# Attention and feed-forward on one core: slots 8 to 31 as four written lists, tail keys as 64-row matmuls with a bank per head

## The chip, the cores and the metric

The kernel runs on one core of a Trainium2 chip. The metric is the device time of one execution in microseconds (us), here as the median of three runs. The engines of the core run side by side, each through its own queue in order: PE (TensorE, matmuls into PSUM, with PEld its weight loads), ACT (ScalarE), DVE (VectorE), POOL (GpSimd) and SP (SyncE). Work of one engine that needs another's result waits on a semaphore. PSUM is used here in units of one bank (512 float32 values in each of 128 partitions).

## The reference

Eight batches, eight heads, 576 positions of 64 values, attention with a bias by distance, then a feed-forward block in which two products are multiplied with each other:

```
scores = scale * np.matmul(q, k.transpose(0, 1, 3, 2))
scores = scores + bias.transpose(2, 0, 1)[None, :, :, :]
scores = scores - np.max(scores, axis=-1, keepdims=True)
attn = np.exp(scores)
attn = attn / (np.sum(attn, axis=-1, keepdims=True) + 1e-09)
attn_out = np.matmul(attn, v).astype(np.float32)
...
x = np.ascontiguousarray(attn_out.transpose(0, 2, 1, 3)).reshape(B * S, H * D)
a = x @ w_a
b = x @ w_b
return (a * b @ w_out).astype(np.float32)
```

x has 4608 rows of 512; w_a and w_b are 512 x 1536, w_out is 1536 x 512. Matmuls take bfloat16 operands.

## The kernel before, in words

**Units of attention.** The work goes in 32 pairs of heads, p = 0 to 31 (p // 4 is the batch, p % 4 the pair of heads in it). The 576 positions are four tiles of 128 (t, 512 "main" positions) and a tail of 64. Scores stand with keys on the partitions and queries along the row. The two heads of a pair (hh = 0 and 1) lie on partitions 0 to 63 and 64 to 127, so a score matmul uses 64 rows of the array.

For a pair p of 8 or more:
- `qk(p, t0)` makes main scores: per tile t two 64-row matmuls of 512 columns into a two-bank tile of pool `ps_sc` (two buffers). With t0 == 2 it also makes the "rows", the scores of main keys against the 64 tail queries: eight 64-row matmuls of 64 columns (L424), head 0 into the bank `trb`, head 1 into a bank of pool `ps_av`.
- `ex(p, t)` on ACT takes the exponential of two banks at once into `at` (L439), `ex_rows` that of the rows into `att` (L431). `mul` (L444) and `mul_rows` (L539) on DVE multiply by the exponential of the bias.
- `qk_tail(p)` makes the scores of tail keys (both heads, 128 rows; 512 and 128 columns, L488 and L489), `ex_tail` (L515) and `mul_tail` (L531) follow.
- `av_mm(p, jqs)` makes the weighted values for query tiles jq = 0 to 4 (4 is the tail): for each a matmul of 130 columns over the tail keys of both heads (L568; in `vt` each head's values stand on its own 64 partitions with zeros on the other 64), then four matmuls of 65 columns per head over the main keys (L578), or, for jq = 4, four of 130 columns (L572). Column 65 of each head holds ones, so it gives the sum for the division.
- `av_norm(p, jqs)` on DVE takes the reciprocals (L589) and multiplies into `XG` (L591, L596). `t_x(p)` has SP transpose `XG` into `xn_sb`, the input of feed-forward.

**Units of feed-forward.** A chunk of 512 rows is 36 units of four matmuls of 512 columns: 24 units (12 x a and b: `ff_in` L642, then on ACT a copy `ha` L649, or on DVE the product `g` L652) and 12 units of output (`ff_o_mm` L679, four row tiles of three units, then on ACT the copy `ob` L684 and the DMA to `out`). Their banks come from pool `ps_ff` (two buffers).

**Order.** The scheduler is off (`manual_schedule`): each engine runs in the order of the program text. An opening of written tokens does p = 0 to 7 and the first chunk's part. Then a loop over slots s = 8 to 32 (L868) does, in slot s, scores, exponentials and multiplies of p = s and weighted values of p = s - 1, in the order of `steps`; nine feed-forward units per slot are put where `U` stands, whole units, with ACT's and DVE's part of a unit right behind its matmuls. In a slot the weighted values stand in two blocks, jq 0 to 2 and jq 3 to 4. Slot 32 has no new scores. The rest of the units comes after the loop. Loads from DRAM (POOL's queue) and the transposes of a batch (SP's queue) are put at the start of certain slots.

Of the kernel before, what the change touches and what calls it, by code (L numbers as in the profile page):

```python
# [13 lines left out]
def kernel(  # L14
# [11 lines left out]
    nc = tc.nc  # L26
# [7 lines left out]
    NM = 4  # L34
# [370 lines left out]
    def shared(p):  # L405
        return p >= 8

    def qk(p, t0, ts=None):
        qT, kT, _ = operands(p)
        st[p].setdefault("at", [None] * NM)  # L410
        for t in ts or (t0, t0 + 1):
            ps = ps_sc.tile([128, 2, 512], FP32, tag="sc", name=f"qk{p}_{t}")
            for hh in range(2):
                r = slice(64 * hh, 64 * hh + 64)
                nc.tensor.matmul(out=ps[:, hh, :], lhsT=kT[r, t, :], rhs=qT[r, :, :],  # L415
                                 start=True, stop=True)
            st[p]["ps", t] = ps
        if shared(p) and t0 == 2:
            z = operands(p)[2]
            rows = (trb.bitcast(FP32), ps_av.tile([128, 512], FP32, tag="av", name=f"qr{p}"))  # L420
            for t in range(NM):
                for hh in range(2):
                    r = slice(64 * hh, 64 * hh + 64)
                    nc.tensor.matmul(out=rows[hh][:, ST * t:ST * t + ST], lhsT=kT[r, t, :],  # L424
                                     rhs=z[r, 0, ST * hh:ST * hh + ST], start=True, stop=True)
            st[p]["rows"] = rows
# [99 lines left out]
    def mul_tail(p):  # L526
        if not shared(p):
            mul_rows(p)
        at, wt = st[p]["att"], Wt_sb[:, p % 4, :]
        o = 512 + main_tail(p) - 128  # L530
        nc.vector.tensor_tensor(out=at[:, o:o + 256], in0=at[:, o:o + 256], in1=wt[:, 255::-1], op=MULT)  # L531

    def mul_rows(p):
        at, w = st[p]["att"], W_sb[p % 4]
        x = at[:, 0:512].rearrange("p (t h c) -> p h t c", h=2, t=NM)
        rev = w[:, :, ST - 1::-1]
        e = bass.AP(tensor=rev.tensor, offset=rev.offset,
                    ap=[rev.ap[0], rev.ap[1], [1, NM], rev.ap[2]])
        nc.vector.tensor_tensor(out=x, in0=x, in1=e, op=MULT)  # L539
# [19 lines left out]
    def av(p, jqs):  # L559
        av_mm(p, jqs)  # L560
        av_norm(p, jqs)

    def av_mm(p, jqs, pool=None, tag="av"):
# [16 lines left out]
                                     stop=True, skip_group_check=True)  # L580
        st[p]["pav", jqs[0]] = pav

    def av_norm(p, jqs):
        pav = st[p]["pav", jqs[0]]
        rc = wrk.tile([128, 3, 2], FP32, tag="rc", name=f"rc{p}_{jqs[0]}")
        xg = XG[p % 2]
        n = len(jqs)
        r = rc[:, 0:n, :]
        nc.vector.reciprocal(out=r, in_=pav[:, 0:n, :, Dh])  # L589
        m = n - (jqs[-1] == 4)  # L590
        nc.vector.tensor_tensor(  # L591
            out=xg[:, jqs[0]:jqs[0] + m, :, :], in0=pav[:, 0:m, :, 0:Dh],
            in1=rc[:, 0:m, :].unsqueeze(3).to_broadcast([128, m, 2, Dh]), op=MULT)
# [127 lines left out]
    def put_units(n):  # L721
        nonlocal nxt
        for _ in range(n):
            units[nxt]()
            nxt += 1

    def v_next(s):
        if s % 4 == 0:
            v_in(s // 4, 0, 4)
        if s % 4 == 2:  # L730
            v_in(s // 4, 4, 8)
# [132 lines left out]
        step(token)  # L864
    pad_tl(1)

    load_slot = {bb: 9 if bb == 3 else 12 if bb == 4 else 4 * bb - 5 for bb in range(3, B)}
    for s in range(8, NP + 1):  # L868
        new = s < NP
        U = "unit"  # L870
        A = lambda *jq: (lambda: av(s - 1, jq) if s > 8 else None)
        steps = []
        if new:
            steps += [lambda: (qk(s, 0), ex(s, 0))]
        if new:
# [12 lines left out]
        else:  # L888
            ff["late"] = True
            steps += [A(0, 1, 2), U, U, U, A(3, 4), lambda: t_x(s - 1, (0, 1, 2)), U, U, U,  # L890
                      lambda: t_x(s - 1, (3, 4)), U, U, U]
        b = s // 4 + 1
        if s % 4 == 2 and b < B:
            t_half(b, 0)
        if s % 4 == 0 and 2 <= b - 1 < B:
            t_half(b - 1, 1)
        if s % 4 == 1 and 2 <= b < B:
            load_vt(b)
        for bb in range(3, B):
            for g in range(2):  # L900
                if s == load_slot[bb] + (2 - (bb < 5)) * g:
                    load_half(bb, g)
        quota = 9
        seen, put = 0, 0
        nu = sum(1 for x in steps if x is U)
        for x in steps:
            if x is U:
                seen += 1
                n = (quota * seen + nu - 1) // nu - put
                put_units(n)  # L910
                put += n
            else:
                x()
    put_units(len(units) - nxt)


# [28 lines left out]
```

## Time and profile before

| What | Value |
|---|---|
| median of 3 runs | 413.77 us |
| lowest and highest run | 412.71 and 413.79 us |
| span of the profiled execution | 412.1 us |
| instructions in it | 8718 |
| slots 9 to 31, first score matmul to the next slot's | 11.00 to 11.01 us each |
| exponentials of main scores (L439), ACT | 112 x 1029 ns |
| multiplies of `at` (L444), DVE | 112 x 685 ns |
| 65-column weighted values (L578), PE | 896 x 193 ns from `at`, 128 from the opening's |
| tail-key weighted values (L568), PE | 152 x 221 ns from `att`, 8 from `atk` |

The span is the time from the first to the last instruction of one profiled execution. A matmul's duration in the profile includes its way through the array, on which the next one follows, so the duration is longer than what it takes of the engine's time: the distance from start to start tells that. Some matmul records are missing in the trace. Views used below: the page (busy shares, the clock granted to TensorE in 40 slices, the chain that ended last), the timeline (instructions in order of time, equal ones merged), the table of stages (busy time per engine in given stretches) and the list of waits.

### The profile page before, as it was taken

How to read it: one execution, taken by the hardware profiler on the slowest of the kernel's cores; microseconds unless marked ns; L12 is line 12 of the kernel's file. 1: busy time of each engine (PE TensorE's matmuls, PEld its weight loads, DVE VectorE, ACT ScalarE, POOL GpSimd, SP SyncE). 2: the span in 40 equal slices, each digit the busy share in tenths (PEclk: the TensorE clock that was granted, in tenths of full speed). 3: DMA queues.
4: the chain of work that ended last, by engine and by line, in shares of the span. 5: the costliest groups of instructions: out<-in, count | busy, mean ns of one | idle time of the engine just before them, and what ended most of it. 6: DMA issues, size and time to landing. Idle time of an engine off the chain costs nothing.

```text
span 412.1 us, 8718 instructions
## 1 busy us (share of the span) xinstructions
PE 401.5 (97%) x3420; PEld 209.6 (51%) x3471; DVE 240.6 (58%) x568; ACT 252.0 (61%) x386; POOL 131.4 (32%) x188
## 2 busy tenths in 40 slices
PE   7999999999999999999999999999999999999996
PEld 3476656455554555455445555555445454444443
DVE  4799997366755765476646764567547652421320
ACT  5898992577748665667557765767476642322321
POOL 5966466887029400960069004300000000000000
PEclk9999999999999999999999999999999999999999
DMA  9999999999969924994199908960520012002004
GB/s 152 185 204 197 206 137 148 166 184 131 91 127 157 141 40 91 151 127 94 35 159 150 120 17 136 117 92 17 117 67 17 16 40 78 0 5 98 2 2 102
DMA packets 135962, 42.36 MB, mean 103 GB/s; under 512 B 113544, under 2 KB 131176, under 8 KB 135920
## 3 DMA queue, kind: packets, MB, share of 16 engines
q0 software_dynamic: 81120, 19.88, 54.9%
q1 hardware_dynamic: 49456, 12.61, 19.9%
q10 hardware_dynamic: 5344, 9.31, 7.1%
q8 instruction: 27, 0.44, 0.5%
q14 instruction: 15, 0.12, 0.1%
HBM read 39.23 MB, written 9.45 MB: 118 GB/s over the span
## 4 chain that ended last, share of the span: by engine, by line
PE 95%; DMA 1%; ACT 1%; issue 1%; DVE 0%; ACTq 0%; SPq 0%
PE pb L642 23%; PE pa L642 23%; PE po L679 22%; PE av L578 8%; PE qk L415 7%; PE av L568 2%; PE av L572 2%; PE qkh L455 1%; PE qkt L488 1%; DMA xn<-in_k_dram 1%; PE trb L330 1%; PE trb L424 1%; PE trk L330 1%; ACT ath L461 0%; PE qkt L494 0%
## 5 line engine op out<-in xcount | busy, mean ns | idle before, releaser
L439 ACT ACTIVATE at<-qk 128x1024 bf16<-128x1024 f32 x112 | 113.4, 1029 | 27.4 <-DMA out_dram<-ob 10.3
L652 DVE TENSOR_TENSOR g<-pb,ha 128x512 bf16<-128x512 f32 (+1 forms) x114 | 75.6, 663 | 74.8 <-PE pb L642 58.5
L642 PE MATMUL pb<-xn,wb 128*128 128x512 bf16 (+1 forms) x440 | 111.1, 368 | 0.8
L642 PE MATMUL pa<-xn,wa 128*128 128x512 bf16 (+1 forms) x440 | 110.8, 368 | 0.7
L649 ACT ACTIVATE ha<-pa 128x512 f32<-128x512 f32 (+1 forms) x114 | 66.3, 581 | 67.6 <-PE pa L642 63.8
L679 PE MATMUL po<-wo,g 128*128 128x512 bf16 x403 | 95.5, 379 | 0.8
L444 DVE TENSOR_TENSOR at<-at,W 128x1024 bf16<-128x1024 bf16 x112 | 75.0, 685 | 22.4 <-ACT at L439 22.3
L642 PEld LDWEIGHTS <-wa 128*128 128x128 bf16 x456 | 41.2, 98 | 46.6 <-issue 6.8
L642 PEld LDWEIGHTS <-wb 128*128 128x128 bf16 x456 | 40.6, 98 | 42.9 <-issue 4.7
L679 PEld LDWEIGHTS <-g 128*128 128x128 bf16 x420 | 38.8, 98 | 44.9 <-issue 2.5
L684 ACT ACTIVATE ob<-po 128x512 f32<-128x512 f32 x34 | 20.4, 600 | 40.2 <-PE po L679 30.1
L578 PE MATMUL av<-vm,at 128*128 128x65 bf16 x896 | 41.2, 193 | 0.0
L578 PEld LDWEIGHTS <-at 128*128 128x128 bf16 x896 | 37.4, 97 | 6.1
L174 POOL DMA_DIRECT2D vt<-in_v_dram x12 | 7.4, 622 | 101.9 <-PE av L572 101.1
L136 POOL DMA_DIRECT2D qn<-in_q_dram x48 | 36.6, 825 | 9.2 <-PE trb L501 6.9
L589 DVE RECIPROCAL rc<-av 128x6 f32<-128x6 f32 (+1 forms) x64 | 11.9, 186 | 45.7 <-PE av L578 41.1
L145 POOL DMA_DIRECT2D kn<-in_k_dram x48 | 36.2, 800 | 2.6 <-DMA qn<-in_q_dram 1.6
L568 PE MATMUL av<-vt,att 128*128 128x130 bf16 x152 | 33.6, 221 | 0.2
L415 PE MATMUL qk<-QB,KB 64*128 64x512 bf16 x192 | 29.1, 381 | 0.3
L591 DVE TENSOR_TENSOR XG<-av,rc 128x384 bf16<-128x384 f32 (+2 forms) x64 | 27.2, 425 | 2.2
L515 ACT ACTIVATE att<-qkt 128x640 bf16<-128x640 f32 x24 | 16.8, 701 | 13.0 <-PE qkt L489 13.0
L568 PEld LDWEIGHTS <-att 128*128 128x128 bf16 x152 | 14.9, 98 | 6.4
(105 smaller groups left out, 322.8 us busy)
## 6 DMA issues: line engine op xcount, KB each, us to landing
out_dram<-ob ACTq DMA_DIRECT2D x31, 256.0 KB, 2.9
vn<-in_v_dram POOLq DMA_DIRECT2D x16, 256.0 KB, 5.7
kn<-in_k_dram POOLq DMA_DIRECT2D x48, 64.0 KB, 4.9
qn<-in_q_dram POOLq DMA_DIRECT2D x48, 64.0 KB, 4.1
wa<-in_moe_w_a_dram POOLq DMA_DIRECT2D x3, 512.0 KB, 8.9
wb<-in_moe_w_b_dram POOLq DMA_DIRECT2D x3, 512.0 KB, 8.3
wo<-in_moe_w_out_dram POOLq DMA_DIRECT2D x1, 1536.0 KB, 15.7
xn<-XG SPq DMA_TRANSPOSE x52, 3.5
```

What stands on the lines that cost most here:

```text
L136: nc.gpsimd.dma_start(out=by_tile(qn[b % 2])[:, h0 // 4, t, :, :], in_=q[b, h0:h1, 128 * t:128 * t + 128, :].transpose([1, 0, 2]))
L145: nc.gpsimd.dma_start(out=by_tile(kn[b % 2])[:, h0 // 4, t, :, :], in_=k[b, h0:h1, t:SM:NM, :].transpose([1, 0, 2]))
L415: nc.tensor.matmul(out=ps[:, hh, :], lhsT=kT[r, t, :], rhs=qT[r, :, :], start=True, stop=True)
L439: nc.scalar.activation(out=at[:, :, :], in_=ps[:, :, :], func=ACTF.Exp, scale=scale)
L444: nc.vector.tensor_tensor(out=at[:, :, :], in0=at[:, :, :], in1=w[:, :, S - 1 + t:S - 1 + t - SM:-1], op=MULT)
L568: nc.tensor.matmul(out=pav[:, slot, :, :], lhsT=weights_tail(p, jq), rhs=vt[i][:, :, hp, :], start=True, stop=True)
L578: nc.tensor.matmul(out=pav[:, slot, hh, :], lhsT=weights(p, t, hh, jq), rhs=vm[i][:, 2 * hp + hh, t, :], start=False, stop=True, skip_grou ...
L591: nc.vector.tensor_tensor(out=xg[:, jqs[0]:jqs[0] + m, :, :], in0=pav[:, 0:m, :, 0:Dh], in1=rc[:, 0:m, :].unsqueeze(3).to_broadcast([128, ...
L642: nc.tensor.matmul(out=ps[:, 0:n], lhsT=w[df // 4][:, mc, 128 * (df % 4):128 * (df % 4) + 128], rhs=xn_sb[mc][:, 512 * c + lo:512 * c + lo ...
L649: nc.scalar.activation(out=ha[:, 0:n], in_=ff["pa", df, lo][:, 0:n], func=ACTF.Copy)
L652: nc.vector.tensor_tensor(out=g_sb[df][:, lo:lo + n], in0=ff["pb", df, lo][:, 0:n], in1=ff["ha", df, lo][:, 0:n], op=MULT)
L679: nc.tensor.matmul(out=po[:, :], lhsT=g_sb[df][:, 128 * tt:128 * tt + 128], rhs=wo_sb[:, df, :], start=(df == 0), stop=(df == NDF - 1))
```

## The change

The loop over slots is replaced by four lists of tokens, `steady[s % 4]`, for s = 8 to 31. A token is one operation or a count of single matmuls: Qt scores of tile t, R the rows, K the tail keys' scores, E, ER, EK exponentials, M, MR, MK multiplies, TL the tail keys' weighted values, A so many matmuls of the other weighted values, Nh the normalisation of head h (with N1 also `t_x`), F so many feed-forward matmuls, H, G, O, D the copy `ha`, the product `g`, the copy `ob` and the output DMA of a unit, V the copy of values. A prime means p = s - 1.

The tail keys' weighted values (`av_tails`) become ten matmuls of 64 rows and 65 columns, head 0 into one bank and head 1 into another. The main keys' weighted values (`av_head`) are 40 matmuls of 65 columns, jq = 4 now per head too, first all of head 0, then of head 1, taken one by one between feed-forward matmuls. The two banks are the same as those of the rows (`two_banks`). Normalisation is per head (`norm_head`). p = 31 is still done by `av`, after the lists. In the new file the new matmuls are L595 (tails), L605 (others), L429 (rows), L942 and L949 (feed-forward), the new normalisation L614 to L618.

```diff
-    trb = ps_tr.tile([128, 1024], BF16, tag="tr", name="trb")
+    trb = [ps_tr.tile([128, 1024], BF16, tag="tr", name="trb")]
     turn = [0]
 
     def tr_half():
         turn[0] ^= 1
-        return trb[:, 512 * turn[0]:512 * turn[0] + 512]
+        return trb[0][:, 512 * turn[0]:512 * turn[0] + 512]
+
+    def two_banks(name):
+        return (ps_tr.tile([128, 512], FP32, tag="tr", name=f"{name}_0"),
+                ps_av.tile([128, 512], FP32, tag="av", name=f"{name}_1"))
...
-        if shared(p) and t0 == 2:
-            z = operands(p)[2]
-            rows = (trb.bitcast(FP32), ps_av.tile([128, 512], FP32, tag="av", name=f"qr{p}"))
-            for t in range(NM):
-                for hh in range(2):
-                    r = slice(64 * hh, 64 * hh + 64)
-                    nc.tensor.matmul(out=rows[hh][:, ST * t:ST * t + ST], lhsT=kT[r, t, :],
-                                     rhs=z[r, 0, ST * hh:ST * hh + ST], start=True, stop=True)
...
+    def qk_rows(p):
+        _, kT, z = operands(p)
+        st[p]["rows"] = rows = two_banks(f"qr{p}")
+        for t in range(NM):
+            for hh in range(2):
+                r = slice(64 * hh, 64 * hh + 64)
+                nc.tensor.matmul(out=rows[hh][:, ST * t:ST * t + ST], lhsT=kT[r, t, :],
+                                 rhs=z[r, 0, ST * hh:ST * hh + ST], start=True, stop=True)
...
+    J = Dh + 1
+
+    def av_tails(p):
+        b, hp = divmod(p, 4)
+        st[p]["av2"] = banks = two_banks(f"av{p}")
+        for jq in range(5):
+            for hh in range(2):
+                r = slice(64 * hh, 64 * hh + 64)
+                nc.tensor.matmul(out=banks[hh][:, J * jq:J * jq + J], lhsT=weights_tail(p, jq)[r, :],
+                                 rhs=vt[b % 2][r, hh, hp, :], start=(jq == 0), stop=True,
+                                 skip_group_check=True)
+
+    def av_head(p, hh):
+        b, hp = divmod(p, 4)
+        bank, v = st[p]["av2"][hh], vm[b % 2]
+
+        def mm(jq, t):
+            w = weights_last(p, t) if jq == 4 else weights(p, t, hh, jq)
+            return lambda: nc.tensor.matmul(out=bank[:, J * jq:J * jq + J], lhsT=w,
+                                            rhs=v[:, 2 * hp + hh, t, :], start=False, stop=True,
+                                            skip_group_check=True)
+
+        return [mm(jq, t) for jq in range(5) for t in range(NM)]
+
+    def norm_head(p, hh):
+        x = st[p]["av2"][hh][:, 0:5 * J].rearrange("p (j d) -> p j d", d=J)
+        rc = wrk.tile([128, 5], FP32, tag="rc2", name=f"rh{p}_{hh}")
+        nc.vector.reciprocal(out=rc[:, :], in_=x[:, :, Dh])
+        nc.vector.tensor_tensor(out=XG[p % 2][:, 0:4, hh, :], in0=x[:, 0:4, 0:Dh],
+                                in1=rc[:, 0:4].unsqueeze(2).to_broadcast([128, 4, Dh]), op=MULT)
+        rows = slice(ST * hh, ST * hh + ST)
+        nc.vector.tensor_tensor(out=XG[p % 2][0:ST, 4, hh, :], in0=x[rows, 4, 0:Dh],
+                                in1=rc[rows, 4:5].to_broadcast([ST, Dh]), op=MULT)
...
     def ff_o_out(c, tt):
+        ff_ob(c, tt)
+        ff_store(c, tt)
+
+    def ff_ob(c, tt):
         ob = ob_last if (c, tt) == (0, 2) else wrk.tile([128, DM], FP32, tag="ob", name=f"ob{c}_{tt}")
         nc.scalar.activation(out=ob[:, :], in_=ff["po", tt][:, :], func=ACTF.Copy)
+        ff["ob", tt] = ob
+
+    def ff_store(c, tt):
+        ob = ff["ob", tt]
...
+    steady = {
+        1: """
+            Q0 TL' Q1 A5 F1 A2 E0 A7 F1 A2 F1 A1 F1 A1 F1 H0 A2 F1 N0' A2 F1 E1 A2 F1 A3 F1 G1 A1
+            F1 A1 F1 A1 F1 M1 A7 H2 A2 F1 A1 F1 N1' F3 Q2 G3 Q3 E2 R M0 F4 H4 F3 E3 K G5 F3 M2 F2
+            H6 F1 M3 F2 EK F2 ER F1 MK F1 G7
+        """,
+        2: """
+            Q0 H8 Q1 MR' TL' E1 A5 F1 A2 F1 A1 F1 E0 A1 F1 A4 F1 G9 A4 F1 A2 F1 M1 A2 F1 A3 F1 H10
+            N0' A1 F1 A1 F1 A2 F1 A1 F1 A1 G11 A2 F1 A3 F1 A3 F1 A2 F1 H12 N1' F3 Q2 V Q3 G13 E2 R
+            F4 M2 F1 H14 F3 E3 K G15 F3 EK M0 F2 ER F1 MK F1 M3 H16
+        """,
+        3: """
+            Q0 Q1 MR' TL' A2 F1 A1 F1 A1 G17 A8 F1 A2 F1 A2 F1 A1 F1 H18 A3 F1 N0' A1 F1 E0 A2 F1
+            A2 F1 G19 A4 F1 E1 A4 F1 A5 F1 A2 F1 H20 N1' F3 Q2 G21 Q3 E2 R F1 M0 F3 M2 F1 H22 F2 K
+            E3 F3 G23 F1 EK F2 M1 ER F2 MK F1 M3 F2
+        """,
+        0: """
+            Q0 MR' Q1 TL' A3 F1 A2 F1 A1 F1 O26 A1 F1 A4 F1 E1 A2 F1 A2 F1 A2 F1 D26 A1 F1 A2 E0 F1
+            N0' A3 F1 A3 F1 A6 F1 A2 F1 A2 F1 O29 A2 F1 A1 F1 A1 D29 F1 N1' F3 Q2 M1 Q3 E2 R F4 ER
+            M2 F2 E3 K MR F1 V F2 M0 EK F3 O32 MK F1 M3 F2 D32 F2 O35 D35
+        """,
+    }
...
+    def ff_part(n):
+        c, u, m = 1 + (n // 4 - 48) // 36, (n // 4 - 48) % 36, n % 4
+        if u < 24:
+            df, (w, kind) = u // 2, ((wa_sb, "pa"), (wb_sb, "pb"))[u % 2]
+            if m == 0:
+                ff[kind, df, 0] = ff_bank(f"{kind}{c}_{df}")
+            nc.tensor.matmul(out=ff[kind, df, 0][:, :], lhsT=w[df // 4][:, m, 128 * (df % 4):128 * (df % 4) + 128],
+                             rhs=xn_sb[m][:, 512 * c:512 * c + 512], start=(m == 0), stop=(m == NMC - 1))
+        else:
+            tt, part = divmod(u - 24, 3)
+            if part == 0 and m == 0:
+                ff["po", tt] = ff_bank(f"po{c}_{tt}")
+            df = 4 * part + m
+            nc.tensor.matmul(out=ff["po", tt][:, :], lhsT=g_sb[df][:, 128 * tt:128 * tt + 128],
+                             rhs=wo_sb[:, df, :], start=(df == 0), stop=(df == NDF - 1))
+        if m == 3 and (u < 24 or u % 3 == 2):
+            ff["done"][u] = c
...
+    ff["skip"] = 108 - sum(int(x[1:]) for k in (1, 2, 3) for x in steady[k].split() if x[0] == "F")
+
+    def slot_step(s, token):
+        name, num = token.rstrip("'0123456789"), "".join(x for x in token if x.isdigit())
+        if name in ("F", "A"):
+            for _ in range(int(num)):
+                if name == "F" and ff["skip"] > 0:
+                    ff["skip"] -= 1
+                elif name == "F":
+                    ff_part(ff["mm"])
+                    ff["mm"] += 1
+                elif av_queue:
+                    av_queue.pop(0)()
...
+        if name == "Q":
+            qk(p, 0, (i,))
+        elif name == "TL":
+            av_tails(p)
+            av_queue[:] = av_head(p, 0) + av_head(p, 1)
+        elif name == "R":
+            qk_rows(p)
...
+        elif name == "N":
+            norm_head(p, i)
+            if i == 1:
+                t_x(p)
...
-    for s in range(8, NP + 1):
-        new = s < NP
-        U = "unit"
-        A = lambda *jq: (lambda: av(s - 1, jq) if s > 8 else None)
-        steps = []
-        if new:
-            steps += [lambda: (qk(s, 0), ex(s, 0))]
-        if new:
-            head = [U, lambda: ex(s, 1), A(0, 1, 2), U, lambda: mul(s, 0), U,
-                    lambda: mul(s, 1)]
-            late = [A(3, 4), lambda: t_x(s - 1), U]
-            if s == 8:
-                late = [U]
-            pair = [lambda: v_next(s), lambda: (qk(s, 2), ex(s, 2), ex_rows(s)), U,
-                    lambda: ex(s, 3), U, lambda: mul(s, 2), lambda: mul_rows(s)]
-            tail = [lambda: (qk_tail(s), ex_tail(s)), U, U, lambda: mul_tail(s)]
-            if s % 4 == 0:
-                steps += head + late + [U] + pair + [lambda: mul(s, 3)] + tail
-            else:
-                steps += head + pair + late + [U, lambda: mul(s, 3)] + tail
-        else:
-            ff["late"] = True
-            steps += [A(0, 1, 2), U, U, U, A(3, 4), lambda: t_x(s - 1, (0, 1, 2)), U, U, U,
-                      lambda: t_x(s - 1, (3, 4)), U, U, U]
+    while ff["skip"] < 0:
+        ff_part(ff["mm"])
+        ff["mm"] += 1
+        ff["skip"] += 1
+    for s in range(8, NP):
...
-        quota = 9
-        seen, put = 0, 0
-        nu = sum(1 for x in steps if x is U)
-        for x in steps:
-            if x is U:
-                seen += 1
-                n = (quota * seen + nu - 1) // nu - put
-                put_units(n)
-                put += n
-            else:
-                x()
+        for token in steady[s % 4].split():
+            slot_step(s, token)
...
+    nxt = ff["mm"] // 4
+    ff["late"] = True
+    trb[0] = ps_tr.tile([128, 1024], BF16, tag="tr", name="trz")
+    p = NP - 1
+    av(p, (0, 1, 2))
+    put_units(3)
+    av(p, (3, 4))
+    t_x(p, (0, 1, 2))
+    put_units(3)
+    t_x(p, (3, 4))
```

More of the change, by code (lines that the diff above doesn't have):

```diff
@@ L417, in qk @@
             st[p]["ps", t] = ps
-        if shared(p) and t0 == 2:
-            z = operands(p)[2]
-            rows = (trb.bitcast(FP32), ps_av.tile([128, 512], FP32, tag="av", name=f"qr{p}"))
-            for t in range(NM):
-                for hh in range(2):
-                    r = slice(64 * hh, 64 * hh + 64)
-                    nc.tensor.matmul(out=rows[hh][:, ST * t:ST * t + ST], lhsT=kT[r, t, :],
-                                     rhs=z[r, 0, ST * hh:ST * hh + ST], start=True, stop=True)
-            st[p]["rows"] = rows
+    def qk_rows(p):
[6 more added lines that the diff above has]
+                                 rhs=z[r, 0, ST * hh:ST * hh + ST], start=True, stop=True)
     def ex_rows(p):
@@ new lines @@
+    ff["done"] = {}
+    ff["mm"] = 4 * nxt
+    ff["skip"] = 108 - sum(int(x[1:]) for k in (1, 2, 3) for x in steady[k].split() if x[0] == "F")
[10 more added lines that the diff above has]
+                    av_queue.pop(0)()
+            return
+        if name in ("H", "G", "O", "D"):
+            u = int(num)
+            if u not in ff["done"]:
+                return
+            c = ff["done"][u] if name in ("H", "G", "O") else ff["done"].pop(u)
+            if name == "H":
+                ff_ha(c, u // 2, 0, 512)
+            elif name == "G":
+                ff_g(c, u // 2, 0, 512)
+            elif name == "O":
+                ff_ob(c, (u - 24) // 3)
+            else:
+                ff_store(c, (u - 24) // 3)
+            if name in ("H", "G"):
+                del ff["done"][u]
+            return
+        name, i = token.rstrip("'0123"), "".join(x for x in token if x.isdigit())
+        i = int(i) if i else 0
+        p = s - token.endswith("'")
+        if p < 8:
+            return
+        if name == "Q":
[5 more added lines that the diff above has]
+            qk_rows(p)
+        elif name == "K":
+            qk_tail(p)
+        elif name == "E":
+            ex(p, i)
+        elif name == "ER":
+            ex_rows(p)
+        elif name == "EK":
+            ex_tail(p)
+        elif name == "M":
+            mul(p, i)
+        elif name == "MR":
+            mul_rows(p)
+        elif name == "MK":
+            mul_tail(p)
+        elif name == "N":
+            norm_head(p, i)
+            if i == 1:
+                t_x(p)
+        elif name == "V":
+            v_next(p)
+        else:
+            raise ValueError(token)
@@ L892 @@
+    av_queue = []
+    load_slot = {bb: 9 if bb == 3 else 12 if bb == 4 else 4 * bb - 5 for bb in range(3, B)}
+    while ff["skip"] < 0:
[3 more added lines that the diff above has]
+    for s in range(8, NP):
         b = s // 4 + 1
@@ L902 @@
                     load_half(bb, g)
-        quota = 9
-        seen, put = 0, 0
-        nu = sum(1 for x in steps if x is U)
-        for x in steps:
-            if x is U:
-                seen += 1
-                n = (quota * seen + nu - 1) // nu - put
-                put_units(n)
-                put += n
-            else:
-                x()
+        for token in steady[s % 4].split():
+            slot_step(s, token)
+    for token in steady[0].split():
+        if token.endswith("'") and token[0] in "EM":
+            slot_step(NP, token)
+    while ff["mm"] % 4:
+        slot_step(NP, "F1")
+    for u in sorted(ff["done"]):
+        for name in (("O", "D") if u >= 24 else ("G",) if u % 2 else ("H",)):
+            slot_step(NP, f"{name}{u}")
+    nxt = ff["mm"] // 4
[8 more added lines that the diff above has]
+    t_x(p, (3, 4))
     put_units(len(units) - nxt)
```

## The prediction

> **What bounds the kernel now.** I read the page first (busy time, granted clock, the chain that ended last), then the waits of TensorE between 94 and 325 us, a table of four slots, and the timeline of one slot.
>
> ```profile
> PE 401.5 (97%) x3420; PEld 209.6 (51%) x3471; DVE 240.6 (58%) x568; ACT 252.0 (61%) x386; POOL 131.4 (32%) x188
> ...
> PEclk9999999999999999999999999999999999999999
> ...
> PE 95%; DMA 1%; ACT 1%; issue 1%; DVE 0%; ACTq 0%; SPq 0%
> ```
>
> TensorE is busy in 97% of the span at the full clock, and the chain of waits is TensorE in 95%. A matmul overlaps the next, so "busy" alone could hide pauses. The table of stages (engines' busy us, then clock, DMA share) is cut at the first score matmul of four slots in a row:
>
> ```profile
> 193.22:204.22 11.00, 10.89 (x94) 5.55 (x96) 7.48 (x17) 6.71 (x10) 0.00 (x0) 1.00 0.08 16
> 204.22:215.23 11.01, 10.90 (x94) 5.55 (x97) 4.76 (x12) 6.77 (x10) 5.49 (x8) 1.00 1.23 148
> 215.23:226.23 11.00, 10.95 (x95) 5.62 (x96) 7.36 (x18) 7.73 (x13) 11.00 (x17) 1.00 1.73 155
> 226.23:237.24 11.01, 10.90 (x94) 5.55 (x96) 7.54 (x18) 7.90 (x12) 0.54 (x1) 1.00 1.20 116
> ```
>
> Every slot takes 11.00 to 11.01 us whatever VectorE (4.8 to 7.5), ScalarE (6.7 to 7.9) and the DMAs do in it. The view of TensorE's waits between 94 and 325 us names no engine at all. So a slot is as long as its matmuls, and I price each by the distance from its start to the next start:
>
> ```profile
> 204.22 0.61 PE L415 MATMUL qk<-QB,KB 64*128 64x512 bf16 x4
> 204.76 1.04 PE L679 MATMUL po<-wo,g 128*128 128x512 bf16 x4
> 205.63 0.22 PE L568 MATMUL av<-vt,att 128*128 128x130 bf16 x1
> 205.69 0.42 PE L578 MATMUL av<-vm,at 128*128 128x65 bf16 x8
> 205.95 0.22 PE L568 MATMUL av<-vt,att 128*128 128x130 bf16 x1
> ...
> 206.33 0.42 PE L578 MATMUL av<-vm,at 128*128 128x65 bf16 x8
> 206.59 1.67 PE L679 MATMUL po<-wo,g 128*128 128x512 bf16 x7
> 208.31 0.22 PE L568 MATMUL av<-vt,att 128*128 128x130 bf16 x1
> ...
> 208.69 0.39 PE L572 MATMUL av<-vm,att 128*128 128x130 bf16 x4
> 208.92 1.89 PE L679 MATMUL po<-wo,g 128*128 128x512 bf16 x8
> 210.74 0.60 PE L415 MATMUL qk<-QB,KB 64*128 64x512 bf16 x4
> 211.19 0.19 PE L424 MATMUL trb<-ZB,KB 64*128 64x64 bf16 x1
> ...
> 211.28 0.19 PE L424 MATMUL qr<-ZB,KB 64*128 64x64 bf16 x1
> 211.40 1.90 PE L679 MATMUL po<-wo,g 128*128 128x512 bf16 x8
> ```
>
> The first four feed-forward matmuls last from 204.76 to 205.63: 0.216 each. Eight 65-column matmuls last from 205.69 to 205.95: 0.0325 each, also where a 512-column one follows (206.33 to 206.59). A 130-column tail matmul (L568) costs 0.06, one of L572 (208.92 - 208.69)/4 = 0.058. The eight 64-row matmuls of L424 start between 211.19 and 211.28: their pairs, one on each half of the rows, are 0.03 apart. Going from 64-row to 128-row work costs extra: four score matmuls from 204.22 to 204.76 are 0.54, where two pairs of 0.22 make 0.44. That is 0.1, and the return to 64 rows costs as much; a slot has four such changes.
>
> **The change, part by part.** It applies to the weighted values of p = 8 to 30, computed in slots 9 to 31: 23 slots. Slot 8 has none, p = 31 is done by the old function, and the opening and the closing feed-forward stay.
>
> Removed per slot: from the timeline, 205.63 to 206.59 and 208.31 to 208.92, together 0.96 + 0.61 = 1.57 us (5 of L568, 32 of L578, 4 of L572).
>
> Added per slot: 10 tail matmuls of 64 rows and 65 columns, which stand in alternation on the two halves and the two banks, like those of L424: 5 pairs of 0.03 = 0.15. And 40 matmuls of 128 rows and 65 columns (32 as before, 8 in place of the four wide ones) at 0.0325 = 1.30. Together 1.45.
>
> So 0.12 us less per slot, 23 x 0.12 = 2.8 us.
>
> Bounds. For the tails: no row shows 64 rows with 65 columns. Below, the pair distance of L424, 0.03; above, no overlap, ten at 0.03 each, 0.30. I take 0.03 a pair, since rows, halves and banks are as in L424. For the 65-column matmuls in the midst of feed-forward: the row of L578 is 0.0325 in a run and ahead of a 512-column one. Below, streaming alone: a 512-column one takes 0.216 and a 128-column one (L489, between feed-forward matmuls at 213.35 and 213.41) 0.056, so 0.42 ns a column and 0.030 for 65. Above, that 0.056. I take 0.0325, the same shape. For changes between 128 and 64 rows: the tails are put between or behind the first two score pairs, which are 64-row too, so there are still four a slot.
>
> The Trainium skill (TensorEngine Tiling, Key Properties) says that a change of tiling mode drains the array; the 0.1 us at each change agrees. It warns here against tails standing among 128-row work: by it two more changes a slot would cost 23 x 0.2 = 4.6 us, and the lists avoid them.
>
> The other parts cost or bring nothing by themselves. Feed-forward stays at 36 matmuls a slot on average (36, 35, 35 and 38 in the four lists). The mixing moves matmuls on an engine that never waits, so it has no wait to remove. VectorE has the same six normalising instructions for a pair; ScalarE's work and the loads keep their slots. The output DMA is issued on ScalarE some steps behind its copy; what stands behind is only ScalarE's, which idles 3 to 4 us a slot.
>
> New waits. Score rows (R) and weighted values now share one pair of banks. R is queued behind Q2 and Q3, and all matmuls behind R. It needs the second normalisation (N1') done. From the last weighted-value matmul to R's start lie 0.033, four feed-forward matmuls (0.86), a change (0.1) and Q2, Q3 (210.74 to 211.19, 0.45): 1.44 us. N1' needs 0.21 until that matmul's result is seen (L578 lasts 193 ns, 0.02 for the signal), a reciprocal (0.23, start to start on VectorE's timeline), a 256-column product (at most 0.47, the start-to-start of the 384-column one there), a 64-row product (0.22), and 0.07 to be seen by TensorE: 1.20. Slack 0.24 us if VectorE is free when N1' is due. In the reverse direction the tails (TL') wait for both exponentials of the rows. From Q2's end in list 1 ScalarE has E2, H4, E3, H6, the tail keys' and two row exponentials: by start-to-start distances on its timeline 0.90 + 0.49 + 0.90 + 0.49 + 0.6 + 0.53 = 3.9. TensorE has Q3, R, two changes, 19 feed-forward matmuls, the tail scores (0.27) and Q0: 0.22 + 0.12 + 0.2 + 4.1 + 0.27 + 0.22 = 5.1, so 1.2 are left for ScalarE's own waits in between. The closest place is H6 of list 1, queued behind E3: adding these distances along the list, the bank that it frees is wanted about 0.02 us after its end. If it is 0.05 late in each of the 6 slots of that list, that is 0.3 us, which I put in.
>
> Sum on the profiled execution: span 412.1 - 2.8 + 0.3 = 409.6. The runs took 412.71 to 413.79, so 0.6 to 1.7 lies around the span; the same difference on the median gives 413.77 - 2.5 = 411.3 us.
>
> **Rivals.**
> 1. The shared banks become the wait (other side). Place: R behind N1'. If VectorE is still in one more multiply of `at` when N1' is due (start to start 0.60 us), R comes 0.60 - 0.24 = 0.36 late, 8.3 us over 23 slots: 411.3 + 8.3 = 419.6. It decides the sign from 0.12 us a slot on. For it: before, only one of their two banks was shared with the weighted values. Against: VectorE is idle in 3.5 us and more of each slot, and the lists put the last multiply or product ahead of N1' at least two feed-forward and several short matmuls earlier.
> 2. A switch between short and long matmuls costs. There are about 15 returns from feed-forward to weighted values a slot (13, 16, 13 and 17 in the lists, against 2 before). If the first short one costs 0.056 like L489, 15 x 0.0235 x 23 = 8.1 us: 419.4. Break-even is 8 ns a switch. The Trainium skill (TensorE: Matmul & The Clock Gate, Part 3: Packing small matmuls) says that weights load beside a running matmul only where its rows differ; that would bare a load at each such switch. Against: from 204.76 to 205.63 four long ones and then a tail cost 4 x 0.216 and no more, and 206.33 to 206.59 shows nothing in the other direction.
> 3. The tails don't overlap: 0.30 in place of 0.15, 23 x 0.15 = 3.5 us: 414.8, no change. This is also what is left if the change doesn't do what it says of 64 rows. Against: L424's pairs overlap, on the same halves.
> 4. Mixed short matmuls stream at 0.030, as their weights are loaded behind a long one: 40 x 0.0025 x 23 = 2.3 us more: 409.0. Against: 0.0325 also ahead of a long one.
>
> **How the numbers follow.** Forecast 0.68, rival 1 0.08, rival 2 0.07, rival 3 0.07, rival 4 0.10. A measurement of this kernel tells 0.3% (1.2 us) from no change: faster is under 412.5, slower over 415.0. Of the forecast's 0.68, 0.64 is faster and 0.04 (H6, or some other late release, eats the half) is no change. Faster: 0.64 + 0.10 = 0.74. Same: 0.04 + 0.07 + 0.01 of rival 1 = 0.12. Slower: 0.07 + 0.07 = 0.14. The range goes from 409.0 (half of rival 4 is below) to 414.8 (rival 3 is in); left out are 0.05 and 0.14.
>
> **What would show it.** Slots of the three lists with 35 or 36 feed-forward matmuls and one with 38 that take together 4 x 10.9 us where they took 44.0; tails in pairs 0.03 apart; short matmuls 0.033 to the next start, also between long ones; no engine named among TensorE's waits. Rival 1 would show as a wait of L429 on VectorE's L618, rival 2 as starts above 0.04 behind L605, rival 3 as ten tails over 0.3 us. I am wrong if slots come out at 11.0 or more.

## The result, and the profile after

The changed kernel takes 410.95 us in the median of six runs (410.52 to 411.61), the kernel before 413.70 in six beside them (412.71 to 413.91). The ratio is 0.9943, with a 95% interval of 0.993 to 0.9955: 2.8 us faster. The forecast was 411.3.

The page of the changed kernel, busy shares, granted clock and the chain that ended last:

```profile
span 409.5 us, 9141 instructions
...
PE 396.5 (97%) x3618; PEld 208.0 (51%) x3678; DVE 242.3 (59%) x568; ACT 252.2 (62%) x386; POOL 131.5 (32%) x188
...
PEclk9999999999999999999999999999999999999999
...
PE 95%; DMA 1%; issue 1%; ACT 1%; DVE 0%; SPq 0%; ACTq 0%
```

TensorE is as much the bound as it was. The table of stages, cut at the first score matmul of four slots (length of the stage first, then busy us of PE, PEld, DVE, ACT, POOL, the clock, DMA share, GB/s):

```profile
180.97:191.60 10.63, 10.52 (x103) 5.41 (x105) 7.73 (x18) 7.34 (x13) 0.00 (x0) 1.00 0.46 91
191.60:202.23 10.63, 10.52 (x102) 5.42 (x103) 7.76 (x17) 7.31 (x12) 0.00 (x0) 1.00 0.19 37
202.23:213.51 11.28, 11.06 (x105) 5.71 (x106) 5.60 (x15) 6.61 (x10) 9.56 (x14) 1.00 1.20 134
213.51:224.37 10.86, 10.75 (x105) 5.45 (x106) 6.46 (x15) 7.89 (x12) 7.60 (x11) 1.00 1.85 159
sum 43.40, PE 42.87 PEld 22.00 DVE 27.56 ACT 29.15 POOL 17.16; mean PE 10.72 PEld 5.50 DVE 6.89 ACT 7.29 POOL 4.29
```

Four slots take 43.40 us in place of 44.02. They differ among themselves because the lists hold 35, 35, 38 and 36 feed-forward matmuls, and they repeat to 0.01 us over the whole stretch: no wait on another engine is in them. TensorE's list of waits between 94 and 325 us (total, times, longest) names no engine either. Its only line is five idle stretches for which the profile shows no cause; a feed-forward record is missing there, as behind 209.26 us:

```profile
PE po L949 <- issue: 0.8, 5, 0.2
```

One slot on TensorE's timeline:

```profile
202.23 0.61 PE L419 MATMUL qk<-QB,KB 64*128 64x512 bf16 x4
202.68 0.32 PE L595 MATMUL av<-vt,att 64*128 64x65 bf16 x10
202.93 0.27 PE L605 MATMUL av<-vm,at 128*128 128x65 bf16 x3
203.03 0.38 PE L949 MATMUL po<-wo,g 128*128 128x512 bf16 x1
203.25 0.22 PE L605 MATMUL av<-vm,at 128*128 128x65 bf16 x2
203.31 0.38 PE L949 MATMUL po<-wo,g 128*128 128x512 bf16 x1
...
204.02 0.29 PE L605 MATMUL av<-vm,at 128*128 128x65 bf16 x4
204.14 0.38 PE L949 MATMUL po<-wo,g 128*128 128x512 bf16 x1
```

The ten tails last from 202.68 to 202.93, 0.25 us, of which 0.1 is the change from 64 to 128 rows, so 0.15 is theirs. Two short matmuls take 0.06 (203.25 to 203.31) and four 0.12 (204.02 to 204.14). These steps of 0.01 are too coarse for the third digit, so I take the single starts of the whole stretch. A short matmul alone between two long ones takes 0.029 us (median), one in a run of two to nine, unless the run stands right behind the tails, 0.0315 to 0.032, and the mean of all is 0.0316. In the kernel before, with runs of eight, the mean is 0.0321.

For the experiments I compare one stretch of the profiled executions, from the first score matmul of slot 9 to that of slot 31 (22 slots). The written lists have one feed-forward matmul (0.22 us) fewer in it than nine units a slot; "a slot" corrects for that. The medians were taken on several chips; each ratio below is against the kernel before on the same chip.

| Kernel | 22 slots, us | a slot against before, us | from TensorE's last matmul to the end, us | median, us |
|---|---|---|---|---|
| before | 242.12 | | 3.93 | 413.70 |
| changed | 238.48 | -0.155 | 4.77 | 410.95 |
| changed, again | 238.48 | -0.155 | 4.13 | 410.75 |
| short matmuls in two runs (`e1_blocks`) | 239.25 | -0.120 | 4.25 | 411.45 |
| loop of units, new weighted values (`e7_oldorder`) | 241.24 | -0.040 | 4.85 | 413.60 |
| tails over all rows (`e2_fullrows`) | 242.01 | +0.005 | 4.82 | 414.86 |
| tails head by head (`e4_nopairs`) | 239.47 | -0.110 | 4.54 | 412.47 |
| tails apart (`e3_apart`) | 243.21 | +0.059 | 4.60 | 415.82 |
| less slack at the banks (`e5_noslack`) | 250.29 | +0.381 | 4.25 | 422.78 |
| last stores on SyncE (`e6_spstore`) | 238.48 | -0.155 | 3.90 | 410.03 |
| eight more small matmuls (`e8_shift`) | 239.30 | -0.118 | 3.91 | 410.61 |
| both (`e9_both`) | 239.31 | -0.118 | 3.89 | 410.43 |

The changed kernel saves 3.42 us until TensorE's last matmul (408.18 against 404.76 us in the spans), and its end takes 0.84 us longer. Both are looked into below.

### The profile page after: what moved, and what is told of

It is laid out like the page before. It is cut to its first block, busy times and chain, and to the rows that moved or that the text cites. A ratio compares the mean times of both kernels' runs of the same rounds, so it can differ in the third digit from the quotient of the medians.

```text
span 409.5 us, 9141 instructions
## 1 busy us (share of the span) xinstructions
PE 396.5 (97%) x3618; PEld 208.0 (51%) x3678; DVE 242.3 (59%) x568; ACT 252.2 (62%) x386; POOL 131.5 (32%) x188
## 4 chain that ended last, share of the span: by engine, by line
PE 95%; DMA 1%; issue 1%; ACT 1%; DVE 0%; SPq 0%; ACTq 0%
PE po L949 15%; PE pa L942 15%; PE pb L942 15%; PE av L605 9%; PE pa L680 8%; PE pb L680 8%; PE qk L419 7%; PE po L717 7%; PE av L582 2%; PE qkt L492 1%; DMA xn<-in_k_dram 1%; PE qkh L459 1%; PE av L595 1%; PE av L572 1%; PE qr L429 1%
## 5 line engine op out<-in xcount | busy, mean ns | idle before, releaser
L690 DVE TENSOR_TENSOR g<-pb,ha 128x512 bf16<-128x512 f32 (+1 forms) x114 | 75.5, 662 | 68.2 <-PE pb L680 40.0
L942 PE MATMUL pa<-xn,wa 128*128 128x512 bf16 x262 | 80.4, 379 | 0.7
L942 PE MATMUL pb<-xn,wb 128*128 128x512 bf16 x278 | 77.8, 379 | 0.0
L949 PE MATMUL po<-wo,g 128*128 128x512 bf16 x277 | 69.7, 379 | 0.8 <-issue 0.8
L605 PE MATMUL av<-vm,at 128*128 128x65 bf16 x736 | 69.0, 194 | 0.6
L605 PEld LDWEIGHTS <-at 128*128 128x128 bf16 x736 | 46.9, 98 | 23.4 <-issue 1.4
L614 DVE RECIPROCAL rh<-av 128x5 f32<-128x5 f32 x46 | 8.9, 194 | 53.4 <-PE av L605 53.4
L949 PEld LDWEIGHTS <-g 128*128 128x128 bf16 x288 | 27.0, 98 | 23.4 <-issue 0.4
L942 PEld LDWEIGHTS <-wb 128*128 128x128 bf16 x288 | 27.0, 98 | 22.7
L680 PE MATMUL pa<-xn,wa 128*128 128x512 bf16 (+1 forms) x165 | 37.8, 349 | 0.2
L680 PE MATMUL pb<-xn,wb 128*128 128x512 bf16 (+1 forms) x164 | 37.7, 348 | 0.2
L942 PEld LDWEIGHTS <-wa 128*128 128x128 bf16 x288 | 26.2, 98 | 16.5
L605 PE MATMUL av<-vm,att 128*128 128x65 bf16 x184 | 24.2, 194 | 0.7
```

Of the source, the lines that this page charges most:

```text
L605: return lambda: nc.tensor.matmul(out=bank[:, J * jq:J * jq + J], lhsT=w, rhs=v[:, 2 * hp + hh, t, :], start=False, stop=True, skip_group_ ...
L680: nc.tensor.matmul(out=ps[:, 0:n], lhsT=w[df // 4][:, mc, 128 * (df % 4):128 * (df % 4) + 128], rhs=xn_sb[mc][:, 512 * c + lo:512 * c + lo ...
L690: nc.vector.tensor_tensor(out=g_sb[df][:, lo:lo + n], in0=ff["pb", df, lo][:, 0:n], in1=ff["ha", df, lo][:, 0:n], op=MULT)
L942: nc.tensor.matmul(out=ff[kind, df, 0][:, :], lhsT=w[df // 4][:, m, 128 * (df % 4):128 * (df % 4) + 128], rhs=xn_sb[m][:, 512 * c:512 * c ...
L949: nc.tensor.matmul(out=ff["po", tt][:, :], lhsT=g_sb[df][:, 128 * tt:128 * tt + 128], rhs=wo_sb[:, df, :], start=(df == 0), stop=(df == ND ...
```

## The experiments

**1. Is it the mixing?** In each list the 40 single matmuls are gathered into two runs, nothing else moves; list 1, for example:

```diff
-            Q0 TL' Q1 A5 F1 A2 E0 A7 F1 A2 F1 A1 F1 A1 F1 H0 A2 F1 N0' A2 F1 E1 A2 F1 A3 F1 G1 A1
-            F1 A1 F1 A1 F1 M1 A7 H2 A2 F1 A1 F1 N1' F3 Q2 G3 Q3 E2 R M0 F4 H4 F3 E3 K G5 F3 M2 F2
-            H6 F1 M3 F2 EK F2 ER F1 MK F1 G7
+            Q0 TL' Q1 F1 E0 A20 F4 H0 F1 N0' F1 E1 F2 G1 F2 A20 F1 M1 H2 F2 N1' F3 Q2 G3 Q3 E2
+            R M0 F4 H4 F3 E3 K G5 F3 M2 F2 H6 F1 M3 F2 EK F2 ER F1 MK F1 G7
```

> The changed kernel with its 40 weighted-value matmuls of a pair in two runs of 20 (one a head) and no longer mixed one by one with feed-forward; nothing else moved. Theory (mixing itself saves, since a 65-column matmul takes about 0.030 us start to start when mixed and 0.0325 in long runs): in the runs 0.0325 again, 40 x about 1.7 ns x 23 = 1.6 us more than the changed kernel, about 412.5 us. Rival (mixing saves nothing, the shorter distance comes from the order of the matmuls or from something else): about 411.0 us and 0.030 inside the runs.

411.45 us, ratio to before 0.994 (0.9926 to 0.9954), which does not differ from the changed kernel's ratio; only the profile tells the two apart. In it a slot is 0.035 us longer than in the changed kernel, 0.8 us in all. On its timeline:

```profile
202.37 0.32 PE L595 MATMUL av<-vt,att 64*128 64x65 bf16 x10
202.62 1.04 PE L945 MATMUL po<-wo,g 128*128 128x512 bf16 x4
203.49 0.67 PE L605 MATMUL av<-vm,at 128*128 128x65 bf16 x16
204.00 0.29 PE L605 MATMUL av<-vm,att 128*128 128x65 bf16 x4
204.34 1.67 PE L945 MATMUL po<-wo,g 128*128 128x512 bf16 x7
```

Sixteen short ones go from 203.49 to 204.00, 0.032 each. (The gap from 204.00 to 204.34 holds a feed-forward matmul whose record is missing.) So mixing saves half of what the theory said, and not all of that in the short matmuls. Their mean is 0.0320 here and 0.0316 mixed, and the difference lies mainly in those that stand alone. About 0.009 us a slot is a small wait that the blocks bring: in list 2 the first matmul into a feed-forward bank starts 0.034 us late, 0.05 us after the end of ScalarE's `ha`. What is left without mixing, 0.120 us a slot, is the count of the prediction to the digit, in part by luck: the short matmuls took 0.0320 and not 0.0325, and this wait and a first feed-forward matmul behind the tails at 0.226 us in place of 0.216 took that gain back.

**2. Is it the order?** The lists are taken out; the loop of whole units of the kernel before stays, with the new weighted values put into it. The rows come after the second head in all slots, since they share its banks.

```diff
+        steps = [lambda: (qk(s, 0), av_tails(s - 1) if s > 8 else None, ex(s, 0))]
+        head = [U, lambda: ex(s, 1), lambda: av_half(s - 1, 0), U, lambda: mul(s, 0), U,
+                lambda: mul(s, 1)]
+        late = [lambda: av_half(s - 1, 1), lambda: t_x(s - 1) if s > 8 else None, U]
+        pair = [lambda: v_next(s), lambda: (qk(s, 2), qk_rows(s), ex(s, 2), ex_rows(s)), U,
+                lambda: ex(s, 3), U, lambda: mul(s, 2), lambda: mul_rows(s)]
+        tail = [lambda: (qk_tail(s), ex_tail(s)), U, lambda: mul_tail(s), U]
+        steps += head + late + [U] + pair + [lambda: mul(s, 3)] + tail
```

> Slots 8 to 31 as a loop of whole feed-forward units like the kernel before, but with the new weighted values (64-row tails behind the first two pairs of score matmuls, a bank per head, 20 matmuls in a run), no written lists. Theory (nothing is gained by the lists as an order, TensorE had no waits to remove; the gain is fewer TensorE cycles of weighted values): 23 x 0.12 = 2.8 us under the kernel before, about 411 us, with up to 0.5 us more for a wait at the tails. Rival (the written order is what gains): 413 us or more.

413.60 us, ratio 0.9994 (0.9981 to 1.0007): nothing gained. The theory falls for this kernel as a whole and holds for its undisturbed slots: these are 10.88 us, 0.12 under before. But 22 x 10.88 is 239.4, and the stretch took 241.24; 1.9 us are waits. Two kinds recur in its trace: tails that wait for VectorE's multiply of `att` (0.14 us), and a feed-forward bank that waits for ScalarE's `ha` (0.10 us). The first on the timeline:

```profile
235.94 0.60 PE L419 MATMUL qk<-QB,KB 64*128 64x512 bf16 x4
236.38 0.46 PE L595 MATMUL av<-vt,att 64*128 64x65 bf16 x10
236.78 1.04 PE L680 MATMUL pa<-xn,wa 128*128 128x512 bf16 x4
```

The tails last 0.40 us in place of 0.25. Its end was long too (4.85 us, see experiment 6), which eats the other 0.9 us in the profiled execution. So the order adds nothing where TensorE did not wait, but the new weighted values, wanted at the very start of a slot, bring waits into the old order, and the lists are free of them.

**3. Are the tails cheaper by their 64 rows?** All 128 rows, with the zeros of the other head, behind the second score pair:

```diff
-                nc.tensor.matmul(out=banks[hh][:, J * jq:J * jq + J], lhsT=weights_tail(p, jq)[r, :],
-                                 rhs=vt[b % 2][r, hh, hp, :], start=(jq == 0), stop=True,
+                nc.tensor.matmul(out=banks[hh][:, J * jq:J * jq + J], lhsT=weights_tail(p, jq),
+                                 rhs=vt[b % 2][:, hh, hp, :], start=(jq == 0), stop=True,
```

> The changed kernel with its ten tail matmuls a pair over all 128 rows (65 columns, zeros in the other head's half), behind the second pair of score matmuls in all lists. Theory: 10 x 0.0325 in place of 0.155 a slot, 23 x 0.17 = 3.9 us more than the changed kernel, about 414.9 us. Rival (64 rows and the overlap of the halves give nothing): about 411 us.

414.86 us, ratio 1.002 (1.0008 to 1.0032). A slot is 0.160 us longer than in the changed kernel (0.17 expected), and the gain of the slots is gone. That the whole time is even above the kernel before (413.94 us beside it) is the longer end, 4.82 us against 3.93.

```profile
204.12 0.60 PE L419 MATMUL qk<-QB,KB 64*128 64x512 bf16 x4
204.65 0.48 PE L594 MATMUL av<-vt,att 128*128 128x65 bf16 x10
204.97 0.26 PE L604 MATMUL av<-vm,at 128*128 128x65 bf16 x3
```

Ten full-row tails last from 204.65 to 204.97, 0.32 us, where the halves took 0.15.

**4. Must the halves alternate?** Five tails of head 0, then five of head 1:

```diff
-        for jq in range(5):
-            for hh in range(2):
+        for hh in range(2):
+            for jq in range(5):
```

> The changed kernel with the ten 64-row tail matmuls in the order five of head 0, then five of head 1, so that neighbours use the same half of the rows and the same bank. Theory (the halves overlap only when they alternate): nearly ten at 0.03 in place of five, 23 x 0.12 to 0.15 = 2.8 to 3.4 us more than the changed kernel, 413.8 to 414.4 us. Rival (the order doesn't matter): about 411 us.

412.47 us, ratio 0.9956 (0.9938 to 0.9973). A slot is 0.045 us longer than in the changed kernel, a third of what was expected.

```profile
203.33 0.61 PE L419 MATMUL qk<-QB,KB 64*128 64x512 bf16 x4
203.77 0.36 PE L595 MATMUL av<-vt,att 64*128 64x65 bf16 x10
204.06 0.27 PE L605 MATMUL av<-vm,at 128*128 128x65 bf16 x3
```

From the first tail to the next work it is 0.29 us (203.77 to 204.06) in place of 0.25. The single starts are 203.770, .799, .807, .831, .847, .861, .881, .890, .911 and .940: after the second, two series about 0.03 apart run side by side. In program order the first five belong to one half, and the two that signal the end of a half are those at .890 and .940, so the second half's tails have started ahead of earlier ones of the first. The expectation that the halves overlap only where they alternate was wrong; alternating is still the better order.

**5. What does a change of rows cost?** One feed-forward matmul is put between the first score pairs and the tails (list 3: `Q0 Q1 MR' F1 TL' A2` in place of `Q0 Q1 MR' TL' A2 F1`).

> The changed kernel with one feed-forward matmul moved between the first score pairs and the tails, so the 64-row tails stand alone among 128-row work. Theory (each change between 64 and 128 rows costs about 0.1 us of TensorE): two more changes a slot, 23 x 0.19 = 4.4 us more than the changed kernel, about 415.3 us. Rival (a change is free and the 0.1 us belongs to the score matmuls): about 411 us.

415.82 us, ratio 1.0062 (1.0041 to 1.0084); a slot is 0.215 us longer than in the changed kernel, the price of two more changes.

```profile
203.97 0.39 PE L949 MATMUL po<-wo,g 128*128 128x512 bf16 x1
204.29 0.33 PE L595 MATMUL av<-vt,att 64*128 64x65 bf16 x10
```

The feed-forward matmul ahead of the tails takes 0.32 us to the next start and not 0.216. The Trainium skill (TensorEngine Tiling (Array Packing), Key Properties) says that changing the tiling mode drains the array. The trace agrees, and it has the price: about 0.1 us each way. The place of the tails, beside the score matmuls, is what lets the change gain.

**The slack at the shared banks.** The three feed-forward matmuls behind N1' are moved behind R, and the product G of their unit with them (list 2: `N1' Q2 V Q3 E2 R F3 G13` in place of `N1' F3 Q2 V Q3 G13 E2 R`).

> The changed kernel with the three feed-forward matmuls between the second normalisation and the next score matmuls moved behind the rows (with the product that hangs on them), so the rows come 0.65 us earlier against the normalisation of the bank that they reuse. Theory (the slack at the shared banks is 0.24 to 0.36 us): TensorE waits 0.29 to 0.41 us a slot for the last product of the normalisation, 23 times, 6.7 to 9.4 us more than the changed kernel, 417.6 to 420.3 us. Rival (the slack is 0.65 us or more): about 411 us.

422.78 us, ratio 1.0224 (1.0205 to 1.0242): more than expected. The timeline and TensorE's list of waits (94 to 325 us; total, times, longest):

```profile
202.39 0.19 PE L429 MATMUL qr<-ZB,KB 64*128 64x64 bf16 x1
202.81 0.29 PE L429 MATMUL qr<-ZB,KB 64*128 64x64 bf16 x7 [0.23 <-DVE XG L618]
```

```profile
PE qr L429 <- DVE XG L618: 4.5, 20, 0.2
```

The second matmul of the rows, into head 1's bank, starts 0.42 us after the first, on the end of the normalisation (L618). Alone they are 0.004 apart, so the wait is 0.41: 0.65 less 0.24, the slack of the prediction. In the trace of the changed kernel the rows start 0.29 us after the normalisation's end; in this one, where they wait for it, 0.06 after, so the slack there is 0.23. The other 0.15 us that such a slot shows in this execution (in three lists of four) is a second wait, of a feed-forward bank for the moved product (`pb` L942 behind `g` L690), which the expectation left out.

**6. Why is the end longer?** ScalarE's part of the end, on the timeline of the kernel before and then of the changed one:

```profile
405.56 0.60 ACT L684 ACTIVATE ob<-po 128x512 f32<-128x512 f32 x1 [1.99 <-PE po L679]
406.19 1.12 ACTq L691 DMA_DIRECT2D out_dram<-ob  x2
407.36 0.38 ACT L320 ACTIVATE ob_last<-po 128x256 f32<-128x256 f32 x1 [1.20 <-PE po L665]
```

```profile
402.15 0.60 ACT L726 ACTIVATE ob<-po 128x512 f32<-128x512 f32 x1 [1.99 <-PE po L717]
402.78 1.97 ACTq L737 DMA_DIRECT2D out_dram<-ob  x2
404.80 0.38 ACT L324 ACTIVATE ob_last<-po 128x256 f32<-128x256 f32 x1 [2.05 <-PE po L703]
```

The same two stores hold ScalarE up for 1.97 us in place of 1.12, the second one 1.46 in place of 0.61, and the copy of the last tile stands behind them. In this trace a 16 KB packet of the instruction queue (a fetch of instructions) runs from 403.42 to 404.38 us, and the slow issue ends at 404.74. In all nine traces with the new weighted values and without the second cure below, this issue ended 0.37 to 0.39 us after such a packet; in the kernel before none fell there. Two cures were tried:

```diff
-                nc.scalar.dma_start(out=out[r0:r0 + ST, :], in_=ob[64 * hh:64 * hh + 64, :])
+                nc.sync.dma_start(out=out[r0:r0 + ST, :], in_=ob[64 * hh:64 * hh + 64, :])
```

> The changed kernel with the output DMAs of the last chunk's first three row tiles issued on SyncE in place of ScalarE. Theory (in the changed kernel the sixth of these issues holds ScalarE up for 1.46 us in place of 0.61, and the last copy behind it starts 0.8 us late): 0.8 us less than the changed kernel, about 410.1 us, and the last copies right behind their matmuls. Rival (the end is not held up by it, or the issue is as slow on SyncE and the end waits there): about 411 us.

```diff
     warm_up(2)
+    for _ in range(8):
+        nc.tensor.matmul(out=warm[:, 0:64], lhsT=zero_sb[:, 0:128], rhs=zero_sb[:, 0:64], start=True, stop=True)
```

> The changed kernel with eight further 64-column matmuls on zeros in the opening, where TensorE waits; their result is not read. TensorE's instruction stream is 16 instructions longer ahead of the end. Theory (the slow issue of the sixth store is a fetch of 16 KB of TensorE's instructions that falls on it, ending 0.37 us before the issue in five traces): the fetch comes about 1.7 us earlier in the work, the issue takes 0.61 us again, 0.8 us less than the changed kernel, about 410.1 us. Rival (the issue is slow by itself at that place): still 1.0 to 1.5 us for that issue, about 411 us.

With SyncE: 410.03 us, ratio 0.9914 (0.9898 to 0.9929), the lowest median of all runs. The slow issue is still there, 1.17 us, now on SyncE where nothing waits behind it, and the end takes 3.90 us as before:

```profile
402.58 1.68 SPq L737 DMA_DIRECT2D out_dram<-ob  x2
403.22 0.38 ACT L324 ACTIVATE ob_last<-po 128x256 f32<-128x256 f32 x1 [0.66 <-PE po L703]
```

With the eight matmuls: 410.61 us, ratio 0.9926 (0.9906 to 0.9946). The packet came earlier in the work (3.67 us ahead of TensorE's last matmul; 1.28 to 1.98 in the nine traces), the issue took 0.615 us, and the end 3.91 us. So the fetch follows TensorE's instruction stream, and with the fetch out of its way the store is not held. Overlap alone does not hold it, though: here the packet, from 402.45 to 403.56 us, meets the last third of the issue before, which runs from 402.05 and still takes 0.614. Part of the gain went elsewhere in this execution:

```profile
PE pa L944 <- DMA xn<-XG: 0.7, 1, 0.7
```

One feed-forward matmul at 216.8 us waited 0.66 us for the transpose that writes `xn`. The wait at the same place is in both profiles that have the eight matmuls, and `e2_fullrows` loses 0.19 us at the same matmul without a named cause, so the lists seem to leave little slack there. Why the transpose came late was not tried.

Both together, with the changed kernel run again beside them:

> The changed kernel again, as it is, beside the next one on the same chip. About 411.0 us, the sixth late store again over 0.9 us to issue.

> The changed kernel with both cures of its end: the last chunk's stores of the first three row tiles on SyncE, and eight more small matmuls in the opening so that the late instruction fetch falls between two stores. Theory: no store takes over 0.65 us to issue, 0.8 to 0.9 us less than the changed kernel on this chip, about 410.0 us; no better than the SyncE stores alone, since the same wait is removed once. Rival (the two add up): 409.3 us.

410.75 us, ratio 0.9923 (0.9908 to 0.9938), for the changed kernel, run again; 410.43 us, ratio 0.9906 (0.9889 to 0.9924), for both cures. The profile shows the end cured in both kernels with SyncE (3.89 and 3.90 us); in whole times the intervals overlap, so a gain over the changed kernel of some 0.5 us is likely, not shown. The changed kernel's second profile had the slow issue at 0.84 us, not over 0.9 as expected, and an end of 4.13: the loss changes from one execution to the next.

## Why the prediction was right, point by point

- **TensorE bounds every slot, and a slot is the sum of its start-to-start distances.** Right. The slots with 35, 36 and 38 feed-forward matmuls take 10.63, 10.85 and 11.28 us, 0.216 us a matmul to within 0.01, and no other engine is waited for.
- **Weighted values 1.57 to 1.45, 0.12 us a slot.** Right in kind and size: 0.120 without the mixing (experiment 1), though its last digit is luck. The 64-row tails are all of it: without them the gain was gone (experiment 3).
- **0.0325 for the mixed short matmuls.** Mis-sized. The term was 40 x 0.0325 = 1.30; at the measured mean of 0.0316 it is 1.26, which is the 0.035 us a slot (0.8 us) that came on top. Half of this is the reading, since before they took 0.0321 on average, and the rest is the mixing. Rival 4 named this with 0.030 and 2.3 us; a third of it came.
- **0.3 us for H6 of list 1.** Not seen: no such wait is in the trace.
- **The end stays.** Wrong by 0.84 us in the profiled execution: an instruction fetch fell on a store. The prediction had no term for it. The short matmuls (+0.8 of gain), H6 (+0.3), this (-0.84) and an opening that was 0.15 us longer in this execution nearly cancel, so it is luck that the 409.6 for the span met 409.5.
- **The lists bring nothing, as there was no wait to remove.** Half right. They remove no old wait, but they keep out 1.9 us of new ones that the new weighted values have in the old order (experiment 2). The prediction walked the lists and not that other case.
- **Rival 1, the shared banks.** It did not come; the slack of 0.24 us was right (0.23), and experiment 5's kernel shows what it would have cost.
- **Rival 2, a price on switches, and rival 3, no overlap.** Neither came. From a feed-forward matmul to a short one behind it are 0.215 us (median of 309 places) as between two feed-forward ones, so no weight load is bared at a switch. Rival 3's "ten at 0.03 each" was too much even as a case: head by head the tails cost only 0.045 us a slot more.

## What to carry to other kernels

Where one engine never waits, price its instructions by the distance from start to start, and look for fewer or shorter ones; an order is then worth what new waits it keeps out. Work on half the rows should alternate between the halves and stand beside other work on half the rows, since each change from half to full rows or back cost TensorE 0.1 us here, as much as three short matmuls. Look at what stands behind the last stores: on a queue with nothing behind it a late issue costs nothing.

## What the hardware showed that was not expected

- Beside a fetch of 16 KB of instructions, the issue of the second of two stores of 64 rows ended only 0.37 to 0.39 us after the fetch (0.84 to 1.55 us for an issue of 0.61), on ScalarE and on SyncE; in these nine cases the fetch had begun before that issue or at most 0.2 us into it. Not held were such an issue where the fetch began 0.34 or 0.39 us into it (`e9_both`, `e8_shift`), the first store of the pair in `e10_after` (0.473 us as elsewhere, with a fetch that began 0.01 us into it), and stores of 128 rows (0.34 us) that met a fetch earlier in the same traces. Transposes issued on SyncE show the same, in the kernel before as well: the one at 209.66 us took 1.95 us in place of 1.20 and ended 0.43 us after a fetch. Why some are held and others not is open.
- 64-row matmuls of the two halves, issued five and five, overlapped out of program order: ten starts within 0.17 us, where two sequences of five at 0.03 would take 0.27.
- A 65-column matmul takes 0.029 us alone between two long ones and 0.0315 to 0.032 in a run of two or more, also of twenty.
